# An early copy of the first V group and a later second softmax in a segment-recurrent attention kernel

## The chip, the cores and the metric

The kernel runs on one core of one Trainium2 chip. The metric is the device time of one launch in microseconds; less is better. Runs of the kernel before gave a median of 1802.4 us, from 1800.01 to 1809.87 us in three runs.

## The reference

Two independent results are computed and concatenated along the last axis. Part A is a gated long convolution over a sequence of 2048 tokens and 1024 channels (a short filter on k, a product with v, a convolution as long as the sequence, a product with q). Part B is an attention with a recurrent memory; the change lies in this part.

```python
mem = mem0                                        # 8 memory rows
for s in range(n_seg):                            # 64 segments of 32 tokens, one after the other
    h = concatenate([mem, x[s*32:(s+1)*32]])      # 40 rows x 1024
    q, k, v = h @ Wq, h @ Wk, h @ Wv              # 32 heads of 128
    p = softmax(where(mask, q @ k.T * scale, -1e9))
    o = (p @ v) @ Wo                              # 40 rows x 1024
    mem = o[:8]                                   # the next segment needs these rows
    outs.append(o[8:])
```

All inputs are bfloat16. A segment can't start before the memory rows of the one before are known, so the 64 segments form one chain, and each of them reads all four weight matrices (1024 x 4096 each).

## The kernel before

About the first 475 us compute part A, and what part B can prepare for all segments at once: keys, queries and values of the last 8 tokens of each segment, kept in a DRAM tile (REC for keys and queries, VBD for values). Then come the 64 segments, in a loop whose order on each engine is written out by hand (`manual_schedule`): every engine executes its instructions in program order, and the framework adds the semaphore waits only.

The weights are cut into 64 chunks of 128 x 2048 (512 KB): 16 for each of K, Q, V and the output projection O, V and the others in two groups `g` of 16 heads. Most chunks stay in SBUF. Sixteen are listed in `STREAM`. Two of them, `KEPT_A` and `KEPT_B`, are kept in unused columns of PSUM (tiles `OTp`, `tps` and `SB`) and copied out of there by VectorE in quarters of 512 columns (`quarter`, `quarter_b`, both through `bits`, L796) shortly before their use. The others are read from DRAM again in every segment into a ring of five buffers (`wring`, issued on SP's queue at L722 and L724). One of these, `PART`, has its first `PART_COLS` columns resident in a tile of its own (`part`), and only the rest is streamed. A ring buffer is refilled when the matmuls of its chunk are through (`done`, then `fetch`).

Within a segment a group of K, Q or V is a `Proj` object: `run(n)` issues the matmuls of the next n chunks into a PSUM bank (L956), and `evac` copies the bank to SBUF on ScalarE (L965). By name the steps around the change are:

- `pv0`, `pv1`: the two groups of V. V0 and V1 are their copies in SBUF.
- `scores(1, QT1, KT1)`: the matmuls of the second group's scores into `SB` (L980 and L983).
- `softmax_a`: VectorE finds the maximum and subtracts it (L989, L991), `seed_scores` writes the mask for the next scores, and ScalarE takes the exponentials (L994).
- `softmax_b`: VectorE sums, divides and transposes (L999 to L1017) into PT.
- `attend(g, PT, V)`: the attention matmuls of one group (L1024 for the segment's own rows, L1028 for the prepared values `VBs[g]`) into `OTp`. `evac_o(g)` copies the result to SBUF on ScalarE (L1036), as `OT0` and `OT1`.
- `out_proj`, `out_half`, `out_quarter`: the output projection, chunk by chunk, into the two banks `yacc` (L1046). Half f = 0 is copied to `Y` first, half f = 1 last (L1142); the projection of chunks in `FIRST` starts with all f = 0 halves.
- `fill_mem`: small matmuls (L901) that turn memory rows of `Y` for the next segment.

SBUF buffers are shared by tags: tiles with the same tag in the pool `one` use one buffer after another, and the later one waits until the earlier is read. Tag "A" holds, in this order, K and Q copies, KT1, V0, V1 and quarters; tag "D" holds the prepared values `VBs[1]`, then a quarter, then `Y`, which the output stores on GpSimd's queue read (L1144). The loads of `VBs` (L933), of the next segment's rows (`load_x`, L882) and of its prepared keys and queries (`load_kq`, L887) stand on GpSimd's queue too.

Of the kernel before, what the change touches and what calls it, by code (L numbers as in the profile page):

```python
# [9 lines left out]
BF = mybir.dt.bfloat16  # L10
# [10 lines left out]

FIRST, LAST = (0, 1, 2, 3), (10, 15, 11, 12, 14)
KEPT_A, KEPT_B = (3, 13, 0), (3, 9, 0)
PART, PART_COLS = (3, 4, 0), 1648
O_ORDER = (*FIRST, 4, 5, 6, 7, 9, 13, 8, *LAST)
ORDER = [(0, kc, 0) for kc in (0, 1, 4, 5)] + [(1, kc, 0) for kc in (0, 1)] + [(0, kc, 0) for kc in (2, 3, 6, 7)] + \
    [(1, kc, 0) for kc in range(2, 8)] + [(m, kc, 1) for m in (0, 1) for kc in range(8)] + \
# [395 lines left out]
def b_kernel(ctx: ExitStack, tc, x, mem0, Wq, Wk, Wv, Wo, outb, n_seg, run_a):  # L423
    nc = tc.nc
# [40 lines left out]
    VBD = dram.tile([2, n_seg, 8, 16, 128], BF, name="VBD")  # L465
# [144 lines left out]
    def evac(dst, src):  # L610
        flip[0] += 1
        if flip[0] % 3 and units[0] < STAGE3:
            nc.scalar.copy(dst, src)
        else:
            nc.vector.tensor_copy(dst, src)
# [163 lines left out]
    one = ctx.enter_context(tc.tile_pool(name="b_one", bufs=1, side="right", reuse_waits="tile"))  # L779
# [6 lines left out]
    OTp = ps_o.tile([128, 4, 512], F32, name="OTp")  # L786
# [14 lines left out]
    def quarter_b(q, tag):  # L801
        t = one.tile([128, 256], I32, tag=tag, name="quarter_b")
        w = []
        for home, at in B_homes[q]:
            n = home.shape[1] * (home.shape[2] if len(home.shape) == 3 else 1)
            bits(like(t[:, at:at + n], home), home)
            part = t[:].bitcast(BF)[:, 2 * at:2 * at + 2 * n]
            for dh, o in enumerate(quarter_cols(q)):
                lo, hi = max(at, 128 * dh), min(at + n, 128 * dh + 128)
                if lo < hi:  # L810
                    w.append((o + 2 * lo - 256 * dh, o + 2 * hi - 256 * dh, part[:, 2 * (lo - at):2 * (hi - at)]))
        return w
# [25 lines left out]
    def quarter(q, tag):  # L838
        t = one.tile([128, 512], BF, tag=tag, name="quarter")
        bits(t[:].bitcast(I32), OTi[:, q, 160:416])  # L840
        return [(o, o + 256, t[:, 256 * dh:256 * dh + 256]) for dh, o in enumerate(quarter_cols(q))]
# [43 lines left out]
    def load_kq(s):  # L885
        rec = one.tile([128, 512], BF, tag="KQ", name="rec_kq")
        nc.gpsimd.dma_start(rec[:], REC[:, s, 256:768])  # L887
        pend_kq[s] = rec[:, 0:256], rec[:, 256:512]
# [18 lines left out]
    with tc.manual_schedule():  # L907
# [18 lines left out]
        for s in range(n_seg):  # L926
# [2 lines left out]
            hT, (KBs, QBs) = pend.pop(s), pend_kq.pop(s)  # L929

            def values(g):
                VB = one.tile([128, 128], BF, tag="D" if g else "VBs", name="VBs")
                nc.gpsimd.dma_start(VB[:], VBD[g, s].rearrange("t h e -> h t e"))  # L933
                return VB

            VBs = [values(0)]
# [7 lines left out]
            class Proj:  # L944
# [15 lines left out]
                    self.kc += n  # L960
                    return self

                def evac(self, tag="A"):
                    sb = one.tile([128, 512], BF, tag=tag, name="qkv_sb")
                    nc.scalar.copy(sb[:], self.acc[:])  # L965
                    return sb

            def transposes(sb, at, tiles=False):
# [18 lines left out]
            def softmax_a(tag):  # L987
                mx = one.tile([128, 8], F32, tag="mx", name="mx")
                nc.vector.tensor_reduce(out=mx[:], in_=S, op=ALU.max, axis=AX.X)  # L989
                E = one.tile([128, 8, 40], F32, tag=tag, name="E")  # L990
                nc.vector.tensor_tensor(out=E[:], in0=S, in1=mx[:].unsqueeze(2).to_broadcast([128, 8, 40]),  # L991
                                        op=ALU.subtract)
                seed_scores()
                nc.scalar.activation(E[:], E[:], ACT.Exp, scale=scale)  # L994
                return E

            def softmax_b(E, tag):
                ssum = one.tile([128, 8], F32, tag="ssum", name="ssum")
                nc.vector.tensor_reduce(out=ssum[:], in_=E[:], op=ALU.add, axis=AX.X)  # L999
                nc.vector.reciprocal(ssum[:], ssum[:])  # L1000
                nc.vector.tensor_tensor(out=ssum[:, 4:8], in0=ssum[:, 4:8], in1=rowhead[:], op=ALU.mult)  # L1001
                nc.vector.tensor_tensor(out=P_pad[:, 0:4, 0:32], in0=E[:, 0:4, 0:32],
                                        in1=ssum[:, 0:4].unsqueeze(2).to_broadcast([128, 4, 32]), op=ALU.mult)
                own = P_pad[:].rearrange("p b k -> p (b k)")[:, 32:320].rearrange("p (i w) -> p i w", w=72)
                nc.vector.tensor_tensor(out=own[:, 0:4, 0:8], in0=E[:, 0:4, 32:40],
                                        in1=ssum[:, 0:4].unsqueeze(2).to_broadcast([128, 4, 8]), op=ALU.mult)
                nc.vector.tensor_tensor(out=E[:, 4:8, :], in0=E[:, 4:8, :],
                                        in1=ssum[:, 4:8].unsqueeze(2).to_broadcast([128, 4, 40]), op=ALU.mult)
                nc.vector.tensor_copy(P_pad[:, 4, 32:64].rearrange("p (i t) -> p i t", i=4), E[:, 4:8, 32:40])
                with nc.allow_low_precision("one of the four terms is not zero"):  # L1010
                    nc.vector.tensor_reduce(out=P_pad[:, 4, 0:32], in_=E[:, 4:8, 0:32].rearrange("p i k -> p k i"),
                                            op=ALU.add, axis=AX.X)
                PT = one.tile([128, 2, 4, 40], BF, tag=tag, name="PT")
                for kb in range(2):
                    ks = slice(32 * kb, 32 * kb + 32)
                    nc.vector.transpose(out=PT[:, kb, :, 0:32], in_=P_pad[:, 0:4, ks])
                    nc.vector.transpose(out=PT[:, kb, :, 32:40], in_=P_pad[:, 4, ks])  # L1017
                return PT

            def attend(g, PT, V):  # L1020
                for i in range(4):
                    cv = slice(i * 128, i * 128 + 128)
                    for c in range(4):
                        nc.tensor.matmul(OTp[:, c, i * 40:i * 40 + 40], lhsT=V[32 * c:32 * c + 32, cv],  # L1024
                                         rhs=PT[32 * c:32 * c + 32, 0, i, :], start=(i == 0), stop=False,
                                         tile_position=(32 * c, 0), skip_group_check=True)
                for c in range(4):
                    nc.tensor.matmul(OTp[:, c, 0:160], lhsT=VBs[g][32 * c:32 * c + 32, :],  # L1028
                                     rhs=PT[32 * c:32 * c + 32, 1].rearrange("p i q -> p (i q)"), start=False, stop=True,
                                     tile_position=(32 * c, 0), skip_group_check=True)  # L1030

# [2 lines left out]
            def evac_o(g):  # L1034
                OT = one.tile([128, 4, 4, 40], BF, tag="B" if g else "C", name="OT")
                nc.scalar.copy(OT[:], o_view)  # L1036
                return OT
# [19 lines left out]
            def out_proj(hps, OT):  # L1057
                for hp in hps:
                    for f in range(2):
                        out_half(hp, f, OT)  # L1060

            def out_quarter(ch, q, w):
                project(2 * ch[1] + q // 2, q % 2, w, OT1)
# [22 lines left out]
            pv0 = Proj(2, 0).run(3)  # L1086
# [2 lines left out]
            QT1 = one.tile([128, 4, 4, 32], BF, tag="B", name="QT")  # L1089
            nc.scalar.copy(QT1[:], turned_q)  # L1090
            nc.scalar.copy(KT1[:, :, :, 0:32], turned_k)
            pv0.run(5)
            pv1 = Proj(2, 1).run(1)
            scores(1, QT1, KT1)
            V0 = pv0.evac()
            E1 = softmax_a("B")
            pv1.run(2)
            attend(0, PT0, V0)
            OT0 = evac_o(0)
            PT1 = softmax_b(E1, "B")  # L1100
            pv1.run(5)
            if not last:
# [3 lines left out]
            for f, hps in enumerate((FIRST, FIRST[-1:] + FIRST[:-1])):  # L1106
                for hp in hps:
                    out_half(hp, f, OT0)
            out_proj((4,), OT0)
            attend(1, PT1, V1)  # L1110
            OT1 = evac_o(1)
            qs = {}
            if s == 0:
                out_proj((5, 6, 7), OT0)
                load_kq(s + 1)
                out_proj((9, 13, 8), OT1)
                steps = {}
            else:
                qs["B", 0], qs["A", 0], qs["A", 2] = quarter_b(0, "KQ"), quarter(0, "A"), quarter(2, "D")
                out_proj((5, 6, 7), OT0)  # L1120
                qs["B", 2] = quarter_b(2, "C")
                out_quarter(KEPT_B, 0, qs["B", 0])
                if not last:
                    load_kq(s + 1)
                out_quarter(KEPT_A, 0, qs["A", 0])
                qs["A", 1] = quarter(1, "A")
                out_proj((8,), OT1)
                steps = {(0, 0): [("A", 2)], (0, 1): [("B", 2), ("B", 1, "C")], (0, 2): [("A", 1), ("A", 3, "A")],
                         (1, 0): [("B", 1), ("B", 3, "C")], (1, 1): [("A", 3)], (1, 3): [("B", 3)]}
            for f, hps in enumerate((LAST, LAST[-1:] + LAST[:-1])):  # L1130
                for n, hp in enumerate(hps):
                    if f == 1 and n == 3 and not last:
# [84 lines left out]
```

## Time and profile before

| | |
|---|---|
| median of the runs | 1802.4 us (1800.01 to 1809.87) |
| profiled execution | 1805.56 us, its span 1803.8 us |
| mean granted TensorE clock | 0.984 |
| busy TensorE (matmul) | 1687.1 us |
| busy VectorE | 1071.1 us |
| busy ScalarE | 658.8 us |
| busy GpSimd | 339.1 us |
| DMA | 605.02 MB, mean 335 GB/s |

The times of the profile are microseconds from the span's start. A timeline row gives start, duration, engine, line, operation, output<-inputs and, in brackets, how long the engine was idle before and what released it. PE is TensorE's matmul, PEld its weight load, DVE VectorE, ACT ScalarE, POOL GpSimd, SP the queue of SyncE; a q behind the name means the sequencer. Rows of one kind that follow each other are merged (x16: sixteen instructions). In a row of busy time by stage stand, behind the engines, the granted clock, the share of the DMA engines' time that was busy (records can overlap, so that it can pass 1) and GB/s.

### The profile page before, as it was taken

The page shows a single profiled execution, that of the slowest core. Times are in us where ns is not written, and L with a number is a line of the kernel's source. Part 1 is how long each engine was busy: PE and PEld are TensorE (multiplying, and loading weights), DVE is VectorE, ACT ScalarE, POOL GpSimd, SP SyncE. Part 2 cuts the span into 40 slices and gives each one's busy share as a digit, 9 for nine tenths or more (in the row PEclk, how much of TensorE's full clock was granted, in tenths as well). Part 3 has the DMA queues.
Part 4 walks back from the last instruction along what each step waited for, and adds up shares of the span by engine and source line. Part 5 has one row for each costly group of instructions (what it writes and reads, how often), then busy time and mean ns, then how long its engine had stood idle before and what let it go on. Part 6 is the DMA issues. An engine that isn't in the chain of part 4 may idle for free.

```text
span 1803.8 us, 71244 instructions
## 1 busy us (share of the span) xinstructions
PE 1687.1 (94%) x30808; PEld 1001.7 (56%) x30840; DVE 1071.1 (59%) x3492; ACT 658.8 (37%) x1157; POOL 339.1 (19%) x627
## 2 busy tenths in 40 slices
PE   6988997697999999999999999999999999999998
PEld 2443323243666666666666666666666666666665
DVE  9926875333565565566666555666555556555555
ACT  6955650000333333333333333333333333333333
POOL 4103342100111112111111211111112111111111
PEclk9999998798999999999999999999999999999999
DMA  9989987998999999999999999999999999999997
GB/s 345 353 321 299 303 276 265 309 327 326 348 351 338 340 354 354 343 350 343 343 347 346 356 349 342 345 344 345 341 345 345 347 348 344 339 339 342 343 343 280
DMA packets 220927, 605.02 MB, mean 335 GB/s; under 512 B 58482, under 2 KB 66818, under 8 KB 220612
## 3 DMA queue, kind: packets, MB, share of 16 engines
q1 hardware_dynamic: 161092, 532.26, 82.0%
q0 software_dynamic: 20128, 45.13, 7.3%
q10 hardware_dynamic: 39392, 23.07, 4.3%
q8 instruction: 241, 3.95, 0.9%
q14 instruction: 74, 0.61, 0.1%
HBM read 545.31 MB, written 57.67 MB: 334 GB/s over the span
## 4 chain that ended last, share of the span: by engine, by line
PE 76%; DMA 14%; ACT 4%; DVE 3%; issue 2%; ACTq 1%; POOL 0%; SPq 0%; POOLq 0%; DVEq 0%
PE acc L956 33%; PE yacc L1046 23%; DMA wring<-WS 9%; PE kb_ps L624 5%; ACT qkv_sb L965 2%; PE OTp L974 2%; DMA REC<-stage 2%; PE OTp L892 2%; PE OTp L1024 2%; PE s_ps L247 1%; PE ks_ps L285 1%; ACT s_sb L249 1%; ACTq L653 1%; PE SB L980 1%; PE SB L983 1%
## 5 line engine op out<-in xcount | busy, mean ns | idle before, releaser
L1046 PEld LDWEIGHTS <-OT 128*64 128x64 bf16 x8319 | 432.8, 109 | 40.3 <-ACT OT L1036 30.9
L956 PEld LDWEIGHTS <-rec 128*32 128x32 bf16 x12288 | 299.4, 96 | 279.7 <-issue 43.4
L965 ACT CAST qkv_sb<-acc 128x512 bf16<-128x512 f32 x384 | 225.1, 586 | 528.2 <-PE acc L956 326.9
L956 PE MATMUL acc<-Wres,rec 128*32 128x512 bf16 x3328 | 239.3, 381 | 0.9 <-issue 0.8
L956 PE MATMUL acc<-wring,rec 128*32 128x512 bf16 x2300 | 227.9, 383 | 10.3 <-DMA wring<-WS 8.5
L1046 PE MATMUL yacc<-Wmore,OT 128*64 128x256 bf16 (+1 forms) x2560 | 219.4, 274 | 0.1
L956 PE MATMUL acc<-Wmid,rec 128*32 128x512 bf16 x3072 | 211.9, 379 | 1.6 <-issue 1.6
L1046 PE MATMUL yacc<-wring,OT 128*64 128x256 bf16 (+1 forms) x2192 | 184.1, 271 | 2.2 <-DMA wring<-WS 2.0
L1142 ACT CAST Y<-yacc 128x256 bf16<-128x256 f32 x128 | 47.7, 373 | 257.9 <-PE yacc L1046 257.9
L796 DVE TENSOR_SCALAR quarter<-OTp 128x256 int32<-128x256 int32 x252 | 99.9, 417 | 64.5 <-ACT OT L1036 64.5
L1036 ACT CAST OT<-OTp 128x640 bf16<-128x640 f32 x128 | 87.4, 683 | 131.2 <-PE OTp L1028 131.2
L956 PE MATMUL acc<-pw,rec 128*32 128x512 bf16 x1796 | 134.2, 380 | 0.9 <-issue 0.7
L933 POOL DMA_DIRECT2D VBs<-VBD x128 | 69.2, 540 | 296.6 <-DVE mx L989 76.1
L1075 DVE COPY KT<-OTp 128x512 bf16<-128x512 bf16 x64 | 27.2, 425 | 153.5 <-PE OTp L892 153.5
L956 PE MATMUL acc<-Wlate,rec 128*32 128x512 bf16 x1536 | 116.5, 379 | 0.0
L1144 POOL DMA_DIRECT2D out_dram<-Y x128 | 65.7, 513 | 233.1 <-ACT Y L1142 227.6
L989 DVE TENSOR_REDUCE mx<-SB 128x8 f32<-128x320 f32 x128 | 62.9, 491 | 67.6 <-PE SB L983 65.8
L994 ACT ACTIVATE E<-E 128x320 f32<-128x320 f32 x128 | 60.1, 469 | 78.1 <-DVE E L991 77.1
L903 DVE CAST rec<-tps 128x32 bf16<-128x32 f32 x128 | 24.5, 192 | 106.6 <-PE tps L901 106.6
L624 PE MATMUL kb_ps<-XBT,pw 128*128 128x512 bf16 x314 | 82.8, 402 | 2.8 <-DMA pw<-in_B_Wk_dram 1.1
L882 POOL DMA_DIRECT2D rec<-REC x64 | 36.1, 564 | 261.6 <-DVE ssum L1001 248.8
L1046 PE MATMUL yacc<-Wlate,OT 128*64 128x256 bf16 x1024 | 78.8, 276 | 0.1
(221 smaller groups left out, 2687.6 us busy)
## 6 DMA issues: line engine op xcount, KB each, us to landing
wring<-WS SPq DMA_DIRECT2D x831, 512.0 KB, 6.0
SK<-s_sb SPq DMA_DIRECT2D x16, 512.0 KB, 4.6
SU<-s_sb SPq DMA_DIRECT2D x16, 512.0 KB, 6.4
Kg<-SK SPq DMA_DIRECT2D x32, 256.0 KB, 4.5
Ug<-SU SPq DMA_DIRECT2D x32, 256.0 KB, 5.5
REC<-stage ACTq DMA_DIRECT2D x16, 512.0 KB, 11.4
zt<-SZ SPq DMA_DIRECT2D x16, 512.0 KB, 7.5
rec_kq<-REC POOLq DMA_DIRECT2D x64, 128.0 KB, 6.3
```

The lines of the kernel that those rows point to most:

```text
L624: nc.tensor.matmul(ps[:], lhsT=ws[kc][:, hl * 128:(hl + 1) * 128], rhs=xbt(kc).rearrange("p s t -> p (s t)"), start=(kc == 0), stop=(kc == 7))
L796: nc.vector.tensor_scalar(out=dst, in0=src, scalar1=0, scalar2=None, op0=ALU.bitwise_or)
L882: nc.gpsimd.dma_start(rec[:], REC[:, s, 0:256])
L933: nc.gpsimd.dma_start(VB[:], VBD[g, s].rearrange("t h e -> h t e"))
L956: nc.tensor.matmul(self.acc[32 * c:32 * c + 32, :], lhsT=hT[:, ch[1], :], rhs=w[:, 512 * c:512 * c + 512], start=(ch == chs[0]), stop=(ch ...
L965: nc.scalar.copy(sb[:], self.acc[:])
L989: nc.vector.tensor_reduce(out=mx[:], in_=S, op=ALU.max, axis=AX.X)
L994: nc.scalar.activation(E[:], E[:], ACT.Exp, scale=scale)
L1036: nc.scalar.copy(OT[:], o_view)
L1046: nc.tensor.matmul(yacc[f][64 * dh:64 * dh + m, x - o:y - o], lhsT=lhsT, rhs=r, start=(h == (0, 2 * FIRST[-1])[f] and x == o), stop=stop, ...
L1142: nc.scalar.copy(Y[:, 256 * f:256 * f + 256], yacc[f][:, 0:256])
L1144: nc.gpsimd.dma_start(bass.AP(outb.tensor, outb.offset + SEG * s * 2048 + 512 * dh, [[2048, 32], [1, 512]]), Y[64 * dh + NM:64 * dh + 40, :])
```

## The change

The copy of V0 goes into a buffer of its own, the upper 512 columns of the `VBs[1]` tile, which grows from 128 to 640 columns; the tag "D" grows with it from 512 to 640, and the resident tile `part` gives up the 128 columns. The copy is issued directly behind the last V0 matmuls, ahead of the second scores. On ScalarE the first attention's copy comes ahead of the second exponentials. The second attention is issued one chunk of the output projection later. The quarters are taken in another order and in other buffers: (KEPT_B, 3) early, (KEPT_A, 0) through tag "D", and none behind the second chunk of half f = 1.

```diff
-PART, PART_COLS = (3, 4, 0), 1648
+PART, PART_COLS = (3, 4, 0), 1520
...
             def values(g):
-                VB = one.tile([128, 128], BF, tag="D" if g else "VBs", name="VBs")
-                nc.gpsimd.dma_start(VB[:], VBD[g, s].rearrange("t h e -> h t e"))
+                VB = one.tile([128, 640 if g else 128], BF, tag="D" if g else "VBs", name="VBs")
+                nc.gpsimd.dma_start(VB[:, 0:128], VBD[g, s].rearrange("t h e -> h t e"))
                 return VB
...
-                def evac(self, tag="A"):
-                    sb = one.tile([128, 512], BF, tag=tag, name="qkv_sb")
-                    nc.scalar.copy(sb[:], self.acc[:])
+                def evac(self, tag="A", sb=None):
+                    if sb is None:
+                        sb = one.tile([128, 512], BF, tag=tag, name="qkv_sb")[:]
+                    nc.scalar.copy(sb, self.acc[:])
                     return sb
...
-                    nc.tensor.matmul(OTp[:, c, 0:160], lhsT=VBs[g][32 * c:32 * c + 32, :],
+                    nc.tensor.matmul(OTp[:, c, 0:160], lhsT=VBs[g][32 * c:32 * c + 32, 0:128],
...
-            pv0.run(5)
+            V0 = pv0.run(5).evac(sb=VBs[1][:, 128:640])
             pv1 = Proj(2, 1).run(1)
             scores(1, QT1, KT1)
-            V0 = pv0.evac()
-            E1 = softmax_a("B")
             pv1.run(2)
             attend(0, PT0, V0)
             OT0 = evac_o(0)
+            E1 = softmax_a("B")
             PT1 = softmax_b(E1, "B")
             pv1.run(5)
...
-            out_proj((4,), OT0)
+            out_proj((4, 5), OT0)
             attend(1, PT1, V1)
             OT1 = evac_o(1)
             qs = {}
             if s == 0:
-                out_proj((5, 6, 7), OT0)
+                out_proj((6, 7), OT0)
...
             else:
-                qs["B", 0], qs["A", 0], qs["A", 2] = quarter_b(0, "KQ"), quarter(0, "A"), quarter(2, "D")
-                out_proj((5, 6, 7), OT0)
+                qs["B", 0], qs["B", 3], qs["A", 0] = quarter_b(0, "KQ"), quarter_b(3, "A"), quarter(0, "D")
+                out_proj((6, 7), OT0)
                 qs["B", 2] = quarter_b(2, "C")
                 out_quarter(KEPT_B, 0, qs["B", 0])
                 if not last:
                     load_kq(s + 1)
+                out_quarter(KEPT_B, 3, qs["B", 3])
+                qs["A", 2] = quarter(2, "A")
+                out_proj((8,), OT1)
                 out_quarter(KEPT_A, 0, qs["A", 0])
-                qs["A", 1] = quarter(1, "A")
-                out_proj((8,), OT1)
-                steps = {(0, 0): [("A", 2)], (0, 1): [("B", 2), ("B", 1, "C")], (0, 2): [("A", 1), ("A", 3, "A")],
-                         (1, 0): [("B", 1), ("B", 3, "C")], (1, 1): [("A", 3)], (1, 3): [("B", 3)]}
+                qs["A", 1] = quarter(1, "D")
+                steps = {(0, 0): [("B", 2), ("B", 1, "C")], (0, 1): [("A", 2), ("A", 3, "A")], (0, 3): [("A", 1)],
+                         (1, 0): [("B", 1)], (1, 1): [("A", 3)]}
```

## Prediction

> **What bounds the kernel now.** I read the page's chain first, then the busy time by stage, then the waits in the steady part, then the timeline of one segment.
>
> ```profile
> PE 76%; DMA 14%; ACT 4%; DVE 3%; issue 2%; ACTq 1%; POOL 0%; SPq 0%; POOLq 0%; DVEq 0%
> ```
>
> The chain that ended last is TensorE for three quarters, with transfers second. So the question is where TensorE stands still, and whether the transfers let it go faster. The waits from 520 to 1790 us:
>
> ```profile
> ACT Y L1142 <- PE yacc L1046: 240.0, 120, 3.1
> ...
> ACT qkv_sb L965 <- PE SB L983: 35.0, 60, 1.1
> ...
> PEld L1046 <- ACT OT L1036: 29.0, 60, 0.6
> ```
>
> Y is copied twice a segment, so 120 waits are 60 segments in 1270 us: 21.17 us each. The second row is the copy of the first V group (V0): in every segment ScalarE holds it back until the second scores are done. The third is the output projection waiting for the first attention's copy. Two segment starts with no transfer wait between them give the floor of a segment:
>
> ```profile
> 992.51 0.40 PE L956 MATMUL acc<-wring,rec 128*32 128x512 bf16 x4
> ...
> 1013.26 0.40 PE L956 MATMUL acc<-wring,rec 128*32 128x512 bf16 x4
> ```
>
> 20.75 us, against 21.17 on average: 0.42 us a segment, 27 us in 64, is time added to this floor, which I put down to weights that arrive late. Whether that grows depends on the transfers:
>
> ```profile
> 520.00:1790.00 1270.00, 1236.00 (x27216) 795.98 (x27208) 748.65 (x2759) 452.30 (x840) 229.57 (x480) 1.00 0.96 345
> ...
> 992.00:1002.00 10.00, 10.00 (x228) 5.08 (x227) 4.24 (x14) 3.44 (x7) 2.69 (x6) 1.00 1.03 398
> 1002.00:1008.00 6.00, 5.64 (x149) 3.50 (x141) 5.53 (x24) 3.04 (x6) 0.57 (x1) 1.00 0.96 322
> 1008.00:1013.00 5.00, 5.00 (x111) 4.79 (x104) 2.95 (x11) 1.06 (x2) 0.54 (x1) 1.00 0.88 288
> ```
>
> The last three columns are clock, DMA share and GB/s. In the first half of a segment (keys and queries) the DMA engines are full at 1.03; in the second (attention, output projection) they fall to 0.96 and 0.88, I take it because the next transfer waits for a buffer to be freed. TensorE's idle time (5.64 of 6.00) lies exactly there, at full clock. The change works in this half.
>
> **The first attention.** What stands around it:
>
> ```profile
> 1001.81 1.04 PE L956 MATMUL acc<-Wres,rec 128*32 128x512 bf16 x16
> 1002.67 0.39 PE L956 MATMUL acc<-wring,rec 128*32 128x512 bf16 x4
> ...
> 1003.06 0.60 PE L956 MATMUL acc<-Wres,rec 128*32 128x512 bf16 x8
> 1004.02 0.28 PE L1024 MATMUL OTp<-PT,qkv_sb 32*128 32x40 bf16 x16 [0.36 <-ACT qkv_sb L965]
> 1004.13 0.23 PE L1028 MATMUL OTp<-PT,VBs 32*128 32x160 bf16 x4
> 1004.30 0.61 PE L956 MATMUL acc<-Wres,rec 128*32 128x512 bf16 x8
> ...
> 1005.56 0.63 PE L1046 MATMUL yacc<-Wlate,OT 128*64 128x256 bf16 x8
> ...
> 1007.66 0.27 PE L1046 MATMUL yacc<-wring,OT 128*64 128x256 bf16 x1
> 1007.87 0.27 PE L1024 MATMUL OTp<-PT,qkv_sb 32*128 32x40 bf16 x16
> 1007.98 0.23 PE L1028 MATMUL OTp<-PT,VBs 32*128 32x160 bf16 x4
> ```
>
> ```profile
> 1002.23 0.59 ACT L1091 COPY KT<-OTp 128x512 bf16<-128x512 bf16 x1
> 1003.38 0.59 ACT L965 CAST qkv_sb<-acc 128x512 bf16<-128x512 f32 x1 [0.56 <-PE SB L983]
> 1004.45 0.47 ACT L994 ACTIVATE E<-E 128x320 f32<-128x320 f32 x1 [0.49 <-DVE E L991]
> 1004.83 0.67 ACT L1036 CAST OT<-OTp 128x640 bf16<-128x640 f32 x1
> 1005.67 0.59 ACT L965 CAST qkv_sb<-acc 128x512 bf16<-128x512 f32 x1 [0.17 <-PE acc L956]
> 1008.31 0.69 ACT L1036 CAST OT<-OTp 128x640 bf16<-128x640 f32 x1 [2.05 <-PE OTp L1028]
> ```
>
> The V0 matmuls end at 1001.81 + 1.04 = 1002.85, yet their copy starts at 1003.38, since its buffer still holds KT. With a buffer of its own it starts 0.11 after the matmuls, as the V1 copy does (its own end at 1005.56, start 1005.67): 1002.96, ScalarE being free since 1002.82. It ends at 1003.55, and the attention can start 0.05 later (now 1003.97 to 1004.02): 1003.60. TensorE's own arrival: chunks come 0.215 apart (0.86 for four, 1001.81 to 1002.67), so it is done with the two at 1003.06 by 1003.49. Before the second attention the last projection matmul starts at 1007.66, a pair takes 0.11, and the attention starts at 1007.87: 0.10 more, which I take as fixed cost of changing between the two kinds of matmul. So arrival is 1003.59, and the attention moves from 1004.02 to 1003.60. **Gain 0.42 there.**
>
> That 0.10 could also be a wait for the softmax; the second attention would then follow its last transpose by 0.14 (1007.73 to 1007.87) instead of 0.05. The Trainium skill's page TensorEngine Tiling (Array Packing), section Key Properties, says that changing the tiling mode (not only the tile) drains the engine; by that rule, with which these rows agree, the 0.10 is a drain, and stays in the changed kernel.
>
> Projection after it: 0.28 for the attention, five chunks of 0.215, 0.10 for the change of kind: 1003.60 + 1.46 = 1005.06, against 1005.56. The copy of its result must be ready by then: the last attention matmuls, now 1004.13, move to 1003.71; 0.23 and a lag of 0.10 (1007.98 + 0.23 to 1008.31) later the copy starts, 1004.04, and ends at 1004.71, since the exponentials no longer stand ahead of it. It is hidden behind the five chunks. **Gain so far 0.50.**
>
> **The price: the second softmax.** The exponentials now queue behind that copy on ScalarE, and all of the second softmax on VectorE behind them.
>
> ```profile
> 1005.05 0.48 DVE L999 TENSOR_REDUCE ssum<-E 128x8 f32<-128x320 f32 x1
> ...
> 1007.56 0.17 DVE L1017 STREAM_TRANSPOSE PT<-P_pad 128x32 bf16<-128x32 bf16 x1
> ```
>
> They start at 1004.73 instead of 1004.45 and end at 1005.20 instead of 1004.92. The sum starts 0.08 to 0.13 later (0.13 now), 1005.28 to 1005.33, so 0.23 to 0.28 late, and the last transpose ends at 1007.96 to 1008.01 instead of 1007.73. The second attention cannot start before about 1008.04. TensorE reaches it at 1005.06 + 2.31 (1005.56 to 1007.87, the five chunks and the change of kind) + 0.44 for the chunk put ahead (2.21 over five) = 1007.81. So it waits 0.23: the softmax is late next, and the extra chunk covers most but not all. Before, attention plus that chunk would be through at 1007.87 + 0.44 = 1008.31; now 1008.04. **What is left of the 0.50: 0.27 a segment**. The low end is 0.18 (a lag of 0.14 behind the last transpose, so 1008.13), the high end 0.32 (the sum 0.05 sooner).
>
> The copy of the second attention starts 0.44 after the first of its matmuls and takes 0.69; now three chunks (1.3 us) hide it, then only two (0.28 + 0.88 = 1.16 against 1.13 + 0.05). That is even, with 0.02 of loss; without it the loss would be a chunk. The new second quarter (KEPT_B, 3) is not in the same accumulator tile as the attention, so VectorE fetches it during that copy; the others shift by one place, each still a chunk ahead of its use. I cost them at nothing; a wrong place would cost up to 0.4 for a copy. load_kq and load_x, on the GpSimd queue, go out earlier with TensorE, and the output stores and VB loads keep their order.
>
> **The end of the segment.**
>
> ```profile
> 1012.12 0.36 DVE L796 TENSOR_SCALAR quarter_b<-tps 128x192 int32<-128x192 int32 x1 [0.30 <-PE yacc L1046]
> ...
> 1012.21 0.39 PE L1046 MATMUL yacc<-Wmore,OT 128*64 128x256 bf16 x4
> ...
> 1012.52 0.23 PE L901 MATMUL tps<-ident,Y 128*64 128x16 bf16 x4
> ```
>
> Four matmuls at 0.11 a pair are through at 1012.43, but fill_mem starts at 1012.52, 0.04 after VectorE has read tps for that quarter (1012.48). In the built program this matmul waits on VectorE; in the changed one, which takes the quarter early, it doesn't. **Gain 0.09.** (If this is a change of kind too, nothing.)
>
> **The transfers.**
>
> ```profile
> wring<-WS SPq DMA_DIRECT2D x780, 512.0 KB, 6.0
> ...
> wring<-WS SPq DMA_DIRECT2D x60, 100.0 KB, 5.1
> ...
> DMA to landing us min/median/max: 4.6/5.5/6.5
> ...
> 993.29 1.11 POOL L1144 DMA_DIRECT2D out_dram<-Y  x2 [3.33 <-ACT Y L1142]
> ```
>
> The part tile gives up 128 columns, so the 100 KB transfer becomes 132: 64 x 32 KB = 2.1 MB, 6.1 us at 345 GB/s if all of it counts, 0 if it falls into the 4 to 12% that are free in the second half. I take 3. The third row is the landing of the output stores: they read the buffer which V0 now takes over, and V0's copy waits for them; issued by 994.4, landed by 1000.9 at the latest, it is 2 us clear of 1002.96.
>
> **The sum.** 64 x 0.27 + 62 x 0.09 - 3 = 17.3 + 5.6 - 3 = 19.9 us, with the 27 us of late weights unchanged. The profiled execution took 1805.56 us (span 1803.8 and 1.8 around it), 3.2 above the median of the runs: 1785.7 there, 1782.5 on the median, 1.1% faster.
>
> **Rivals.** (1) The transfers are the bound and give the gain back: TensorE asks earlier, the ring is not there. For: 0.96 over the whole stretch, 1.03 where it is full, 6.0 us landings that five buffers barely cover. Against: the idle share lies in the second half, where buffers are freed up to 0.5 us earlier. Half given back is 1792 to 1801, all of it 1802.4 + 6.1 = 1808.5. The Trainium skill's page DMA: Bandwidth & Descriptors, section Specifications, puts a core's limit to HBM at about 358 GB/s; the trace disagrees as a hard cap, with 398 over 10 us. (2) The other way: buffers freed earlier keep the DMA engines full, and half of the 27 us of late weights goes too: 1782.5 - 13 = 1769. (3) Slower: V0's copy does not come early, because something else holds it (the stores that it now waits for, or ScalarE's order). Then the attention stays at 1004.02, its copy runs 1004.46 to 1005.13, the exponentials to 1005.62, the sum starts at 1005.73, 0.68 late, and the second attention at 1008.45 to 1008.55 against 1008.31: 64 x 0.19 = 12 us, plus 3 for transfers, minus 5.6: 1812. It decides as soon as the copy starts 0.3 us later than computed. Against it: the stores are 2 us clear. This is also the case that the change doesn't do what it says.
>
> **Chances.** 0.5% (9 us) is about what a measurement of this kernel can tell from no change. Forecast 0.60, rival 2 0.12: faster. Rival 1 0.20 (three fifths of it half given back): within 0.5%. Rival 3 0.08: slower. The range 1768 to 1803 holds forecast, rival 2 and half given back, and leaves out the rest. Mostly of one sign: its own range is 1774 to 1792.
>
> **What would show it.** Right: V0's copy within 0.2 us of its last matmul, the first L1024 close behind its two chunks, the projection 0.5 us nearer to the scores; a wait of 0.2 us on VectorE at the second L1024; no DVE wait at the first L901; a floor segment of 20.4 us and some 20.85 on average. Wrong: longer or more waits on wring (rival 1), a V0 copy still behind L983 (rival 3), a second attention more than 4.7 us behind the first (3.85 now, 4.44 expected), where the gain is gone.

## The result, and the profile after

| | before | after |
|---|---|---|
| median | 1802.88 us (4 runs, 1800.01 to 1809.87) | 1781.38 us (4 runs, 1777.71 to 1784.34) |
| profiled execution, its span | 1805.56, 1803.8 | 1779.6, 1777.8 |
| a segment undisturbed (the shortest, which recurs) | 20.75 us | 20.20 us |
| a segment on average | 21.18 us | 20.83 us |
| the difference: late | 0.43 us | 0.63 us |

The ratio (of the means) is 0.9874 (0.9839 to 0.9909): 1.3% faster. Predicted were 1782.5 us, an undisturbed segment of 20.4, 20.85 on average and an unchanged lateness. That the total came out so close is luck: two steps were wrong in opposite directions by about the same amount. The engines gained more than predicted, and the transfers took more of it back.

The page's chain by engine, then two starts of segments one after the other, then busy time by stage as shown for before (the last three columns are clock, DMA share and GB/s):

```profile
PE 72%; DMA 19%; DVE 4%; ACT 2%; issue 1%; ACTq 1%; POOL 0%; SPq 0%; POOLq 0%; DVEq 0%
```

```profile
1209.53 0.40 PE L956 MATMUL acc<-wring,rec 128*32 128x512 bf16 x4 [0.42 <-DMA wring<-WS]
...
1229.73 0.40 PE L956 MATMUL acc<-wring,rec 128*32 128x512 bf16 x4
```

```profile
520.00:1765.00 1245.00, 1226.85 (x27159) 787.64 (x27157) 743.33 (x2745) 451.49 (x838) 228.60 (x479) 1.00 0.97 353
1209.00:1219.00 10.00, 9.58 (x219) 4.94 (x220) 4.02 (x13) 3.42 (x7) 2.70 (x6) 1.00 1.03 395
1219.00:1225.00 6.00, 6.00 (x158) 3.97 (x149) 5.53 (x24) 3.07 (x6) 0.56 (x1) 1.00 0.98 342
1225.00:1230.00 5.00, 5.00 (x113) 4.46 (x105) 2.93 (x11) 1.23 (x3) 0.54 (x1) 1.00 0.98 306
```

ScalarE's share of the chain has fallen from 4% to 2%, and DMA's has risen from 14% to 19%. The pair of starts is an undisturbed segment of 20.20 us. In the attention stage TensorE is busy 6.00 of 6.00 us, where it was 5.64, and the DMA share of the later stages is 0.98 where it was 0.96 and 0.88.

That same segment around the attention, TensorE, then ScalarE, then VectorE:

```profile
1220.01 0.24 PE L984 MATMUL SB<-KT,rec_kq 128*32 128x160 bf16 x4
1220.08 0.60 PE L956 MATMUL acc<-Wres,rec 128*32 128x512 bf16 x8
1220.62 0.27 PE L1025 MATMUL OTp<-PT,VBs 32*128 32x40 bf16 x16
1220.73 0.23 PE L1029 MATMUL OTp<-PT,VBs 32*128 32x160 bf16 x4
...
1222.09 0.63 PE L1047 MATMUL yacc<-Wlate,OT 128*64 128x256 bf16 x8
...
1224.30 0.62 PE L1047 MATMUL yacc<-Wmore,OT 128*64 128x256 bf16 x8
1224.85 0.27 PE L1025 MATMUL OTp<-PT,qkv_sb 32*128 32x40 bf16 x16
1224.97 0.23 PE L1029 MATMUL OTp<-PT,VBs 32*128 32x160 bf16 x4
```

```profile
1219.92 0.58 ACT L966 CAST VBs<-acc 128x512 bf16<-128x512 f32 x1
1221.02 0.69 ACT L1037 CAST OT<-OTp 128x640 bf16<-128x640 f32 x1 [0.51 <-PE OTp L1029]
1221.61 0.47 ACT L995 ACTIVATE E<-E 128x320 f32<-128x320 f32 x1
```

```profile
1221.84 0.33 DVE L922 CAST SB<-mask 128x160 f32<-128x160 bf16 x1
1222.11 0.48 DVE L1000 TENSOR_REDUCE ssum<-E 128x8 f32<-128x320 f32 x1
...
1224.33 0.17 DVE L1018 STREAM_TRANSPOSE PT<-P_pad 128x32 bf16<-128x32 bf16 x1
1224.42 0.27 DVE L1017 STREAM_TRANSPOSE PT<-P_pad 128x128 bf16<-128x128 bf16 x1
1224.61 0.17 DVE L1018 STREAM_TRANSPOSE PT<-P_pad 128x32 bf16<-128x32 bf16 x1
```

V0's copy (now written to `VBs`) starts before the second scores are through, and the attention follows its two chunks (1220.08 + 0.44) by 0.10. The second attention (1224.85) comes 4.84 us behind the scores' last matmuls (1220.01), where 5.05 was predicted; the transposes of its softmax end at 1224.78, and its first half at 1224.50.

### The profile page after: what moved, and what is told of

The parts are those of the page before. It is cut to its first block, busy times and chain, and to the rows that moved or that the text cites. A ratio compares the mean times of both kernels' runs of the same rounds, so it can differ in the third digit from the quotient of the medians.

```text
span 1777.8 us, 71402 instructions
## 1 busy us (share of the span) xinstructions
PE 1679.5 (94%) x30840; PEld 994.7 (56%) x30840; DVE 1069.2 (60%) x3492; ACT 659.1 (37%) x1157; POOL 338.4 (19%) x627
## 4 chain that ended last, share of the span: by engine, by line
PE 72%; DMA 19%; DVE 4%; ACT 2%; issue 1%; ACTq 1%; POOL 0%; SPq 0%; POOLq 0%; DVEq 0%
PE acc L956 32%; PE yacc L1047 23%; DMA wring<-WS 13%; PE kb_ps L624 5%; PE OTp L975 2%; DMA REC<-stage 2%; PE OTp L892 1%; PE OTp L1025 1%; ACT s_sb L249 1%; PE s_ps L247 1%; ACTq L653 1%; PE vb_ps L765 1%; PE ks_ps L285 1%; PE SB L981 1%; DMA Wmore<-in_B_Wo_dram 1%
## 5 line engine op out<-in xcount | busy, mean ns | idle before, releaser
L1047 PEld LDWEIGHTS <-OT 128*64 128x64 bf16 x8319 | 428.2, 109 | 46.8 <-ACT E L995 25.9
L966 ACT CAST qkv_sb<-acc 128x512 bf16<-128x512 f32 x320 | 187.3, 585 | 498.4 <-PE acc L956 336.1
L1047 PE MATMUL yacc<-wring,OT 128*64 128x256 bf16 (+1 forms) x2256 | 189.5, 271 | 3.4 <-DMA wring<-WS 3.3
L887 POOL DMA_DIRECT2D rec_kq<-REC x64 | 34.7, 543 | 235.2 <-PE yacc L1047 218.0
```

What stands on the lines that cost most here:

```text
L966: nc.scalar.copy(sb, self.acc[:])
L1047: nc.tensor.matmul(yacc[f][64 * dh:64 * dh + m, x - o:y - o], lhsT=lhsT, rhs=r, start=(h == (0, 2 * FIRST[-1])[f] and x == o), stop=stop, ...
```

## The experiments

Every comparison is with runs of the kernel before on the same chip. "Undisturbed" and "average" are segment times read off the starts of all segments in the profile of that run. Two profiles of the changed kernel gave averages of 20.83 and 20.90 (e9 below), so a difference of less than 0.07 between averages says nothing.

**Half of the stream left out (e1, e2).** How much is due to transfers, and what do the engines gain alone? From the third segment on, a streamed chunk loads its first 1024 columns only, and TensorE reads these twice, so that no matmul is left out; `PART` stays as it is. The cut, the same in both kernels (a third part, not shown, makes the projections of K, Q and V read these pieces):

```diff
 # fetch
+            elif s < 2:
+                nc.sync.dma_start(t[:], stream_src(ch))
             else:
-                nc.sync.dma_start(t[:], stream_src(ch))
+                nc.sync.dma_start(t[:, 0:1024], stream_src(ch)[:, 0:1024])
 # pieces
+        if now[0] > 1:
+            return [(0, 1024, live[now[0], ch][1][:, 0:1024]), (1024, 2048, live[now[0], ch][1][:, 0:1024])]
         return [(0, 2048, live[now[0], ch][1][:])]
```

> The kernel before, in which from the third segment on a streamed chunk loads only its first 1024 columns and TensorE reads these twice (so half of the stream is left out, no matmul is). Theory (the transfers made each segment of before 0.42 us longer than its floor of 20.75, and of after 0.63 longer than its floor of 20.20): the late weights go, every segment takes the floor, 62 x 0.42 = 26 us less than before, about 1777. Rival (the 0.42 is not late weights but something on the engines): no change, about 1802.

> The changed kernel with the same cut of the stream (half of each streamed chunk is left out from the third segment on). Theory: segments of 20.20, 62 x 0.63 = 39 us less than after, about 1742, so 35 us below the cut kernel before: the engines' gain is 0.55 a segment, and the transfers take 0.21 of it back. Rival, the sum as it was predicted (engines' gain 0.36 a segment, late weights unchanged): 0.36 x 64 = 23 us below the cut kernel before, about 1754.

Measured: 1777.11 and 1742.38 us (ratios 0.9848, 0.981 to 0.9886, and 0.9645, 0.9613 to 0.9678). Segments took 20.76 and 20.21 on average, the undisturbed times of the whole kernels. In busy time by stage of the cut kernel after,

```profile
520.00:1725.00 1205.00, 1204.74 (x27090) 772.68 (x27084) 744.31 (x2739) 451.72 (x837) 226.98 (x478) 1.00 0.61 195
```

TensorE stands still for 0.3 us in 1205, at a DMA share of 0.61. So all the time above an undisturbed segment is made by the streamed transfers, in both kernels, and the engines' gain is 34.7 us, 0.55 a segment. The theory's 1777 and 1742 held; the prediction's 0.36 a segment, which would give 1754, didn't.

**The exponentials first again (e3).**

```diff
-            attend(0, PT0, V0)
-            OT0 = evac_o(0)
             E1 = softmax_a("B")
+            attend(0, PT0, V0)
+            OT0 = evac_o(0)
```

(The order as issued; `pv1.run(2)` stays ahead.)

> The changed kernel with the second exponentials ahead of the first attention's copy again. Theory (the copy is on the path, the exponentials are not): the copy starts at 1.84 behind the second scores instead of 1.00, the projection 0.5 later, the second attention finds its softmax long done; floor 20.70; with late weights falling back to 0.42, 21.1 a segment, 18 us over after: about 1800. If transfers did not react, 32 us over: 1813. Rival (the prediction's price: the order costs 0.23 at the second attention): the loss is only 0.27 of floor, 17 us at most and about 1790 with the transfers' reaction.

Measured: 1801.25 us, ratio 0.9985 (0.9965 to 1.0005), undisturbed 20.78, average 21.17. TensorE and ScalarE in an undisturbed segment:

```profile
934.51 0.27 PE L1025 MATMUL OTp<-PT,VBs 32*128 32x40 bf16 x16
...
936.56 0.63 PE L1047 MATMUL yacc<-Wlate,OT 128*64 128x256 bf16 x8 [0.51 <-ACT OT L1037]
```

```profile
935.46 0.47 ACT L995 ACTIVATE E<-E 128x320 f32<-128x320 f32 x1 [1.06 <-DVE E L992]
935.84 0.67 ACT L1037 CAST OT<-OTp 128x640 bf16<-128x640 f32 x1
```

The attention is as early as in the changed kernel, but its copy waits for the exponentials, and the projection comes 2.05 us behind the attention instead of 1.47. That is the 0.58 by which the undisturbed segment is longer. The gain is gone (at most 0.35% is left), though the later attention and the new quarters are still in: without the order on ScalarE these runs show no gain from an early V0.

**The order on ScalarE alone (e7).** The kernel before with the attention's copy ahead of the exponentials, V0 as late as it was.

```diff
-            E1 = softmax_a("B")
             pv1.run(2)
             attend(0, PT0, V0)
             OT0 = evac_o(0)
+            E1 = softmax_a("B")
```

> The kernel before with only the first attention's copy ahead of the second exponentials; V0 is still copied behind the second scores. Theory (the loop runs through PART's release; this order moves the projection forward by 0.07 at most, and the second attention's second half back by 0.28, behind PART): floor 21.0, 1800 to 1808. Rival, priced ahead of the result (the attention 0.19 late counts in full): 1812.

Measured: 1817.08 us, ratio 1.0051 (1.0033 to 1.0069), undisturbed 21.03, average 21.31. The second attention now waits for its softmax, first for one half of PT (ready at 1117.31) and then for the other (1117.59):

```profile
1117.00 0.27 PE L1046 MATMUL yacc<-wring,OT 128*64 128x256 bf16 x1
1117.36 0.28 PE L1024 MATMUL OTp<-PT,qkv_sb 32*128 32x40 bf16 x16
1117.65 0.25 PE L1028 MATMUL OTp<-PT,VBs 32*128 32x160 bf16 x4
```

L1024 starts 0.36 behind the last pair instead of 0.21, and L1028 0.29 behind it instead of 0.11. This is near the slower rival of the prediction, but without that rival's later attention, quarters and bytes. It loses 0.5%, as the price of 1812 against 1802 that was given ahead; that the two agree is partly luck, since an undisturbed segment loses 0.28 and an average one 0.13, where the rival's sum had 0.19. My theory of that moment (1800 to 1808, because the loss lies where transfers hide it) fell. With e3 it shows that the early V0 and the order on ScalarE gain only together: without the order 0.15% is left (0.35% to -0.05%), and the order alone, with the second attention where it was, loses 0.5%. The order with the later attention, but a late V0, was not run.

**The second attention one chunk earlier (e4).**

```diff
-            out_proj((4, 5), OT0)
+            out_proj((4,), OT0)
             attend(1, PT1, V1)
...
-                out_proj((6, 7), OT0)
+                out_proj((5, 6, 7), OT0)
```

> The changed kernel with the second attention one chunk earlier again (behind chunk 4, ahead of 5). Theory (the transposes of the second softmax end at 4.77 behind the second scores, just in time for the attention at 4.84): TensorE comes at 4.39 and waits 0.44 for VectorE; floor 20.64, 15 us (with late weights back at about 0.42) to 28 us over after: 1796 to 1809. Rival (the softmax leaves room, the chunk is only a cover for the copy): no change, 1781.

Measured: 1782.64 us, ratio 0.9871 (0.9834 to 0.9908), undisturbed 20.48, average 20.85. Theory and rival were each half right. The wait is there:

```profile
1057.84 0.27 PE L1047 MATMUL yacc<-wring,OT 128*64 128x256 bf16 x2
1058.21 0.28 PE L1025 MATMUL OTp<-PT,qkv_sb 32*128 32x40 bf16 x16
1058.49 0.25 PE L1029 MATMUL OTp<-PT,VBs 32*128 32x160 bf16 x4
```

```profile
1057.98 0.17 DVE L1018 STREAM_TRANSPOSE PT<-P_pad 128x32 bf16<-128x32 bf16 x1
1058.08 0.27 DVE L1017 STREAM_TRANSPOSE PT<-P_pad 128x128 bf16<-128x128 bf16 x1
1058.27 0.17 DVE L1018 STREAM_TRANSPOSE PT<-P_pad 128x32 bf16<-128x32 bf16 x1
```

L1025 starts behind the transposes of the first half (1058.15) and L1029, 0.28 later instead of 0.12, behind those of the second (1058.44). The undisturbed segment is 0.28 longer. But the average (20.85) lies between the two of the changed kernel, and the time is the same: 18 us of TensorE's waiting fit in where weights were late anyway. For a delay of this size, in this place, the transfers and not the engines set the time of the changed kernel.

**The old order of the quarters (e8).** The changed kernel with the quarter copies and their uses in the order of before (the lines marked - in the last part of the change's diff, `out_proj((6, 7), OT0)` kept).

> The changed kernel with the quarters in the order of before. TensorE's floor loses the 0.09 at fill_mem and some 0.25 at the first quarter that needs the second attention's copy, both behind PART's release. Theory (the loop binds, and time lost behind PART's release and ahead of the next segment's place 6 is partly hidden): 1781 to 1790. Rival (the floor binds): 0.34 x 62 = 21 us, 1802.

Measured: 1790.62 us, ratio 0.9912 (0.9881 to 0.9944), undisturbed 20.63, average 20.94. The changed kernel stood at 0.9874 and, run a second time (e9 below), at 0.9846: 7 to 12 us less, the first of which alone is within the intervals. By the profiles an undisturbed segment loses 0.43, 27 us in all, and an average one 0.04 to 0.11. An undisturbed segment shows where:

```profile
913.43 0.30 PE L1047 MATMUL yacc<-quarter_b,OT 128*64 128x256 bf16 x2
913.89 0.30 PE L1047 MATMUL yacc<-quarter,OT 128*64 128x256 bf16 x2 [0.16 <-DVE quarter L796]
```

```profile
913.41 0.75 DVE L796 TENSOR_SCALAR quarter<-OTp 128x256 int32<-128x256 int32 x2 [0.93 <-ACT OT L1037]
```

A pair takes 0.11, so the second pair is 0.35 late: VectorE can't fetch its quarter out of `OTp` before ScalarE has copied the second attention out of there. The other 0.09 is at fill_mem, which starts 0.31 behind its four matmuls as in the kernel before. So the new order of the quarters does more than the 0.09 it was credited with: it also avoids 0.35 that the later attention would have cost with the old order.

**More bytes (e6, e12).** `PART_COLS` 1392, and 1136, instead of 1520.

> The changed kernel with the resident part of PART 128 columns smaller once more: its transfer is 164 KB instead of 132, 2.1 MB more in all. Theory (this transfer is issued when place 29 is released and lands 1 to 2 us before it is needed, outside the loop that binds): no change, 1780 to 1783. Rival (every byte counts): 2.1 MB at 350 GB/s, 6 us, 1787.

> The changed kernel with the resident part of PART 384 columns smaller: its transfer is 228 KB instead of 132, 6.3 MB more in all. If every byte counts (the transfers are the bound, whatever their place): 6.3 MB at 353 GB/s, 18 us over after, about 1798, ratio to before 0.995. If only the transfers ahead of the keys' and queries' chunks bind (PART's is issued when place 29 is released and lands 1 to 2 us before it is needed): 0 to 5 us over after, about 1783, ratio 0.985 to 0.988.

Measured: 1783.72 us, ratio 0.9867 (0.9827 to 0.9908), with 2.1 MB more, which can't be told from none; and 1783.14, ratio 0.9886 (0.9863 to 0.991), with 6.3 MB more. The changed kernel itself, run again on a third chip (e9), stood at 1780.38, ratio 0.9846 (0.9817 to 0.9876).

> The changed kernel itself, for comparison on the same chip as the next two: 0.987 of before.

So 6.3 MB cost 2 to 7 us by the ratios (0.9886 against 0.9874 and 0.9846), the first within the intervals and the second at their edge. 18 us, a ratio 0.010 higher, is ruled out: in this place of the segment most of the bytes' time is hidden. For the 2.1 MB of the change a third of it, 1 to 2 us, is an estimate.

**Streaming chunks that are needed later (e5, e10, e11).** By now I held that the chunks which land last against their use set the time, above all place 29 of the order.

```diff
-STREAM = (0, 6, 13, 19, 24, 29, 35, 40, 45, 51, 52, 54, 56, 57, 58, 63)
+STREAM = (0, 6, 13, 19, 24, 31, 35, 40, 45, 51, 52, 54, 56, 57, 58, 63)   # e5
+STREAM = (0, 6, 13, 19, 25, 31, 35, 40, 45, 51, 52, 54, 56, 57, 58, 63)   # e10
+STREAM = (0, 6, 13, 20, 26, 31, 35, 40, 45, 51, 52, 54, 56, 57, 58, 63)   # e11
```

> The changed kernel with one other chunk streamed: the eighth of the second Q group (place 31 of the order) instead of the sixth (29); the same bytes. Theory now (a segment's time is a loop of transfers: the release of PART's buffer, behind the output projection's fifth chunk, issues the transfer for place 6, the engines are full until place 29 has landed, 0.3 us too late on average, and TensorE goes from there to PART's release): the last of these chunks is needed two chunks, 0.43 us, later, most of the 0.3 us goes, 20.45 to 20.55 a segment, 18 to 24 us below after: 1757 to 1763. Rival (bytes bind, whatever their order: 0.97 of the DMA engines' time is busy): no change, 1781.

> The changed kernel that streams places 25 and 31 instead of 24 and 29 (the same bytes): the second Q group's streamed chunks are needed 0.22 and 0.43 us later. Theory (the chunks that land last against their need set the loop; with place 31 alone 0.45 us a segment were left, place 24 landing just as it is needed): 0.30 to 0.40 left, 20.5 to 20.6 a segment, 15 to 20 us below after. Rival (the bytes bind at 0.98 of the DMA engines' time): as with place 31 alone, 20.65, 12 us below after.

> The changed kernel that streams places 20, 26 and 31 instead of 19, 24 and 29 (the same bytes): needed 0.5, 0.43 and 0.43 us later. Theory: 0.2 to 0.3 left, 20.4 to 20.5 a segment, 20 to 27 us below after. Rival (bytes bind): 12 us below after; or the later needs only move the wait on to places 35 to 45, nothing below after.

Measured: 1774.28 us (0.9828, 0.9776 to 0.9879), 1778.63 (0.9833, 0.9807 to 0.9859) and 1778.58 (0.9839, 0.981 to 0.9869). On the chip of e10 and e11 the changed kernel took 1780.38. None of the three can be told from it, and the average segments (20.65, 20.86, 20.72, against 20.83 and 20.90 for the changed kernel in two profiles) do not fall in step with the later needs. The theory of the single late chunk isn't borne out, and no version was found that is shown to beat the changed kernel.

## Why the prediction was right, and where it was not

- **The first attention, 0.42:** measured 0.42. L1025 comes 0.54 behind the first of its two chunks (1220.08 to 1220.62), L1024 came 0.96 behind. V0's copy does not wait for the stores whose buffer it took: it starts 0.05 behind its matmuls (they end at 1219.87 by the same reading).
- **The projection, 0.50:** measured 0.49 (2.08 behind the scores' last matmuls instead of 2.57). Up to here the mechanism is the predicted one.
- **The price of the softmax, 0.23 a segment: this step failed.** At most 0.02 is there (the projection to the second attention takes 2.76, against 2.31 + 0.44 predicted). Three terms were mis-sized. The exponentials start 0.59 behind the start of the copy ahead of them, not 0.69: ScalarE begins the next instruction 0.10 before the end that its row shows. (The prediction's own rows have it: exponentials at 1004.45 that take 0.47, the copy behind them at 1004.83.) The sum starts 0.03 behind the exponentials (1222.08 to 1222.11), not 0.08 to 0.13: in before the 0.13 was VectorE's own L922 copy, 0.23 from start to start (the row below, and 1005.05). So the sum is 0.04 later relative to the scores (2.10 against 2.06), not 0.23 to 0.28. And the first attention matmuls need only the first half of PT, ready 0.28 before the second; I let them wait for the last transpose. That was 0.2 x 64 = 13 us in favour of the change. The copy in before:

```profile
1004.82 0.33 DVE L922 CAST SB<-mask 128x160 f32<-128x160 bf16 x1
```

- **The 0.10 at the change of kind of matmul:** it stays where no wait can be. In the changed kernel eight matmuls from 1224.30 take 0.44, the attention starts 0.11 later at 1224.85, and its operand had been ready since 1224.50. So it is not the wait for the softmax. Between matmuls of one kind there is no such step: four from 1228.91 and then fill_mem at 1229.13 (rows below), 0.11 a pair. The rows agree with what the prediction cites from the Trainium skill (TensorEngine Tiling (Array Packing), section Key Properties), that changing the tiling mode drains the engine; that the 0.10 is a drain, and not another cost of the change, no run shows.
- **The end of the segment, 0.09:** in the changed kernel fill_mem follows four matmuls by 0.22 instead of 0.31, and no quarter copy stands ahead of it on VectorE:

```profile
1228.91 0.39 PE L1047 MATMUL yacc<-Wmore,OT 128*64 128x256 bf16 x4
1229.13 0.21 PE L901 MATMUL tps<-ident,Y 128*64 128x16 bf16 x4
```

- **Lateness of the weights, unchanged at 27 us: this step failed too.** It rose from 0.43 to 0.63 a segment (0.70 in the second profile, e9), so that about 13 us were given back. The sum held the lateness as a constant, and it reacts. Rival 1 was right in kind, not in size: 13 of 35 us is more than a third, where it had half or all. The runs beside it show the same reaction: what lengthens an undisturbed segment (e3, e4, e8) shortens the lateness (0.39, 0.37 and 0.31). The starts of rows, averaged over 60 segments against an undisturbed one, tell where it gathers: by the first attention, 11 us into the segment, it is 0.41 of the 0.43 in before and 0.51 of the 0.63 in after, and from the start of the output projection on only 0.01 and 0.04 are added. So the weights come late for the keys, queries and values, and hardly in the half that the change works in.
- **The 2.1 MB, 3 us:** 1 to 2 by the estimate from e12.

The sum as it is: 0.55 x 64 = 35 us from the engines, 13 back, 22 left. The medians differ by 21.5 and the profiled executions by 26, of which 4 lie ahead of the second segment (it starts at 465.64 before and 461.34 after; in the second profile of the changed kernel, e9, at 464.88, so that these 4 are chance).

What stays open: which transfers make a segment late. Only the half stream (e1, e2) frees all of it. Neither the place of the late chunks (e5, e10, e11) nor bytes late in the segment (e6, e12) tells how; a delay of 0.58 ahead of the fifth output chunk (e3) costs time, and one of 0.28 behind it (e4) doesn't, but e7's of 0.28, also behind it, does, in a kernel whose undisturbed segment was 0.55 longer.

## What to carry to other kernels

Where two resources are both nearly always busy, as TensorE (1226.85 of 1245.00 us) and the DMA engines (0.97) are here, a segment has two times, an undisturbed one and an average, and an edit can move them by different amounts: forecast both, and take the reaction of the other resource as a term of the sum, not as a constant. When an instruction is put behind another, ask what its consumer had really waited for, and count lags from starts of rows in the trace, since the next row of an engine can start before the one before shows its end. An experiment that takes half of the transfers away and leaves the engines' work as it is tells the two times apart in one run.

## What was not expected of the hardware

ScalarE's rows overlap by about 0.10 us in unbroken sequences (1221.02 + 0.69 against 1221.61), so that the sum of durations overstates a queue of copies. In full stretches of 10 us the DMA engines moved 395 to 398 GB/s, while the average over the segments was 345 and 353.
